# Mean of the SoLU output taken out in place on ScalarE, lower fp16 half made on GpSimd, and a new order of a round

## The chip, the cores and the metric

One core of one Trainium2 chip runs the whole program. The time is device microseconds of one execution. The engines are TensorE (PE in the rows), VectorE (DVE), ScalarE (ACT), GpSimd (POOL) and the DMA queues, the one of SyncE above all (SP).

## What is computed

Three stages in a row on 4608 tokens: chunked attention (chunks of 64, 8 heads of 64), a SoLU layer with layer norm (512 to 1024 to 512), and a mixture of 8 experts with one expert for each token (512 to 1024 to 512). The change is in the middle stage:

```python
h = x @ w_in
e = np.exp(h - h.max(-1))
solu = h * (e / (e.sum(-1) + 1e-9))
mu = solu.mean(-1); var = ((solu - mu) ** 2).mean(-1)
y = ((solu - mu) / np.sqrt(var + 1e-6) * g_ln) @ w_out
```

## The kernel before

Matmuls run in fp16 with every fp32 operand split in two halves: an upper half (the value rounded to fp16) and a lower half (the rest). A product takes three passes: upper by upper, upper by lower, lower by upper.

The first two reference stages are one loop over 36 tiles of 128 tokens, in software pipeline. Every engine works its instructions off in the order in which the program issues them. That order is written out by hand. `START` is a list of single steps for the first tiles (the weights are prepared in it too), with four tiles, 0 to 3, taken through SoLU. `BODY` is the list of one round. In round `i` the entry `um+0` calls step `um` for tile `i`, `mb-2` calls `mb` for tile `i-2`, and so on. The steps that matter here, with the engine that does each:

- `ld` SyncE loads raw q, k, v of a tile (L301, three buffers); `sc` GpSimd scales it (L311); `hq`, `hk` ScalarE and `lq`, `lk` GpSimd split it (L316, L320, L325, L332).
- `qk` TensorE scores; `mx` VectorE row max (L359); `su` VectorE subtracts it (L365); `ex` ScalarE exponential (L372); `sm` VectorE row sum and reciprocal (L377 to L379); `no` GpSimd normalizes (L384); `ph` ScalarE upper half (L406); `pl` VectorE lower half (L411, both inputs in SBUF); `pr` TensorE transpose; `pe` ScalarE eviction (L426); `pv` TensorE; `xh` ScalarE (L450) and `xl` VectorE (L457) split the attention output.
- `ma` TensorE `h` (L471); `hm` VectorE max of `h` (L477), which I call the max; `eh` ScalarE exponential with its sum (L484); `um` VectorE `u = h * e` with its sum, then two small multiplies for the mean, L493 and L494 (L491); `uh` ScalarE upper half of `u` minus mean, the mean as a bias (L513); `sq` ScalarE sum of squares of `u` minus mean (L499); `ul` VectorE lower half (L519); `ud` SyncE transposing DMA of both halves (L524, in `START` part of `ul`); `ss` GpSimd four tiny ops for the inverse deviation; `mb` TensorE second matmul (L537), which waits for the two eviction steps of the tile before since its PSUM tile has one buffer; `ev` ScalarE evictions (L551, L553) and `el` VectorE lower half of them (L559).
- `ro`, `rk`, `pa` rank the tokens by expert once in four tiles; `sA`, `sB` GpSimd scatter two tiles' rows to memory, in two rounds out of four.
- `ya`, `ys`, `yl` (and `yb`, `yt`, `ym`) split one piece of the experts' weights: ScalarE upper half (L274), VectorE lower half (L275, both inputs in SBUF), SyncE store and next load. From round 8 on every round has one piece; a round with `t % 9 < 5` has a second one, up to 40 pieces in all.

`u` and `e` have one buffer, `us` (the two halves of `u`) two, the transposed `uT` three; `h` and the scores have one PSUM tile each. In the last rounds GpSimd also issues three gathers (L183) that wait for scatters of the tiles before.

The third stage, the experts' matmuls (L93), follows; the change touches nothing in it.

Of the kernel before, what the change touches and what calls it, by code (L numbers as in the profile page):

```python
# [12 lines left out]
AF = mybir.ActivationFunctionType  # L13
ALU = mybir.AluOpType
# [5 lines left out]
NTOK, DM, DFF, NE, H, D = 4608, 512, 1024, 8, 8, 64  # L20
# [28 lines left out]

BODY = """  # L50
ev-3 el-3 pe+1 ph+2 pl+2 ya+0 ys+0 yl+0 ma+0 yb+0 yt+0 ym+0 pv+1 qk+3 hq+4 hk+4 xh+1 lq+4 sA+0 lk+4 sB+0 hm+0
eh+0 xl+1 sc+5 mx+3 um+0 uh+0 su+3 ex+3 sq+0 ul+0 mb-2 sm+3 ud+0 pr+2 rk-4 pa-4 ld+6 no+3 ss+0 ro-3
"""


# [6 lines left out]
S_E = 64.0  # L62
# [4 lines left out]
def tile_attention_solu_moe(  # L67
# [12 lines left out]
    V, A, G, T, SP = nc.vector, nc.scalar, nc.gpsimd, nc.tensor, nc.sync  # L80
# [155 lines left out]
    st = {}  # L236
# [51 lines left out]
    with ExitStack() as ab:  # L288
# [199 lines left out]
        def umul(t):  # L488
            (h, _), (e, se) = st.pop(("h", t)), st.pop(("e", t))
            u = u_p.tile([P, 1024], F32, tag="u", name="u", bufs=1)  # L490
            V.scalar_tensor_tensor(out=u, in0=h.rearrange("p a b -> p (a b)"), scalar=S_U / (S_X * S_WI), in1=e,  # L491
                                   op0=ALU.mult, op1=ALU.mult, accum_out=se[:, 1:2])
            V.tensor_scalar(se[:, 2:3], se[:, 1:2], -1.0 / DFF, None, op0=ALU.mult)  # L493
            V.tensor_scalar(se[:, 4:5], se[:, 1:2], -1.0 / (DFF * S_E), None, op0=ALU.mult)  # L494
            st["u", t] = (u, se, e)

        def stats(t):
            u, se, e = st["u", t]
            A.activation(e, u, AF.Square, bias=se[:, 4:5], scale=1.0 / S_E, accum_out=se[:, 3:4])  # L499
            st["se", t] = se  # L500

        def stats2(t):
# [4 lines left out]
            G.tensor_tensor(out=se[:, 7:8], in0=se[:, 6:7], in1=mhalf, op=ALU.pow)  # L507
            st["rr", t] = se

        def uhi(t):  # L510
            u, se, _ = st["u", t]
            us = u_p.tile([P, 2, 1024], F16, tag="us", name="us")
            A.activation(us[:, 0], u, AF.Identity, bias=se[:, 2:3])  # L513
            st["us", t] = us

        def ulo(t):
            u, se, _ = st["u", t]
            us = st["us", t]
            V.scalar_tensor_tensor(out=us[:, 1], in0=u, scalar=se[:, 2:3], in1=us[:, 0], op0=ALU.add, op1=ALU.subtract)  # L519

        def u_tr(t):
            us = st.pop(("us", t))
            uT = u_p.tile([P, 2, FC, P], F16, tag="uT", name="uT", bufs=3)
            SP.dma_start_transpose(out=uT.rearrange("p s f t -> p (s f) t"), in_=us.rearrange("p s f -> p (s f)"))  # L524
            st["uT", t] = uT
# [135 lines left out]
        def fetch(src, j):  # L661
            if wide:
                SP.dma_start(out=words[j].bitcast(src.dtype), in_=src)
            else:
                SP.dma_start(out=words[j][:, 0:1024].bitcast(F32), in_=src)
# [80 lines left out]
        def gate_split(_):  # L746
# [4 lines left out]

        steps = dict(
            ld=load, sc=scale_qv, hi=split_hi, lo=split_lo, qk=qk, mx=smax, su=ssub, ex=sexp, sm=ssum, no=snorm,
            pt=pt_pe, ph=pt_hi, pl=pt_lo, pv=pv, xh=xt_hi, xl=xt_lo, ma=m1, hm=hmax, eh=exph, um=umul, uh=uhi,
            sq=stats, ul=lambda t: (ulo(t), u_tr(t)), ss=stats2, mb=m2, ev=x2_ev, el=x2_lo,
            fi=lambda k: fetch(w_in[:, k], k), wa=win_f32, ws=win_scale, wh=win_hi, wl=win_lo,
            fo=lambda z: fetch(w_out[:, z], 2 + (z + 2) % 4), fg=consts, oa=wout_f32, os=wout_scale, oh=wout_hi, ol=wout_lo, wt=gate_tr, gs=gate_split, gm=gate_mm,
            gE=gate_end, wp=wpiece_load)
# [11 lines left out]
        def send():  # L770
            nonlocal sent
            if sent < routed:
                scatter(sent)
                sent += 1
# [39 lines left out]
        def early_pieces(t, n, f):  # L814
            if FIRST + 4 <= t < NT - 2 and done[0] < AHEAD and (n == 0 or t % 9 < 5):
                f()

        steps.update(
            ph=p_hi, pl=p_lo, pr=p_tr, pe=pt_ev, ul=ulo, ud=u_tr, hq=qv_hi, hk=k_hi,
            lq=qv_lo, lk=k_lo, mb=m2_tile, rk=rank, pa=place_rows,  # L820
            ro=route_rows, sA=lambda t: ok(t + 4) and send(), sB=lambda t: ok(t + 4) and send(),
            ya=lambda t: early_pieces(t, 0, piece_split), ys=lambda t: early_pieces(t, 0, piece_store),
# [2 lines left out]
        for i in range(FIRST, NT + 3):  # L825
            if i - FIRST < NX:
                G.memset(xs[i - FIRST], 0.0)
            for name in BODY.split():
                t = i + int(name[2:])
# [244 lines left out]
```

## Time and profile before

| what | us |
|---|---|
| median of 3 runs | 984.29 (980.61 to 989.86) |
| profiled execution | 983.6 |
| its span | 981.9 |
| TensorE busy | 887.6 (90%) |
| VectorE busy | 530.7 (54%) |
| ScalarE busy | 445.4 (45%) |
| GpSimd busy | 393.6 (40%) |

The rows below give a start in us from the span's start, a duration in us, the engine, the line of the kernel, the operation, output and inputs, and, where the engine had waited, how long and what ended the wait. An instruction can start on an engine a little before the one ahead of it has ended; so costs on a path are read from start to start.

### The profile page before, as it was taken

Reading aid. Unit: us, or ns where it says so; the run is one execution under the profiler, and the core shown is the slowest. Engines: PE = TensorE matmul, PEld = TensorE weight load, DVE = VectorE, ACT = ScalarE, POOL = GpSimd, SP = SyncE. Lnnn points to the kernel's source line nnn. Section 1 sums busy time; section 2 is a strip of 40 time slices with the busy share of each in tenths; the row PEclk is TensorE's granted clock in tenths of the full one; section 3 lists DMA queues with packets and bytes.
Section 4 is the critical chain, followed back from the end, with each engine's and each line's share of the span. In section 5 each row is a group of like instructions: output and inputs, shape, how many; then the busy total and the mean of one; then the engine's idle time right before and its main releaser. Section 6 shows DMA issues by size and latency. Waiting matters only on the chain.

```text
span 981.9 us, 26885 instructions
## 1 busy us (share of the span) xinstructions
PE 887.6 (90%) x11230; PEld 621.1 (63%) x11230; DVE 530.7 (54%) x966; ACT 445.4 (45%) x687; POOL 393.6 (40%) x503
## 2 busy tenths in 40 slices
PE   0476999989998999998998999998999999999997
PEld 0233666656666666665667776676767676777674
DVE  7996468898888888888963522222222221111111
ACT  3663367776777777777652122232222221112121
POOL 2765256656666666665443311112111211221120
PEclk9976999999999999999999999999999999999999
DMA  9377145898779987799679467979799853963234
GB/s 379 126 211 152 37 109 162 241 262 284 199 225 277 266 267 214 211 257 288 190 191 176 156 218 243 230 189 345 228 278 330 207 170 87 342 130 77 67 100 164
DMA packets 170145, 203.27 MB, mean 207 GB/s; under 512 B 131868, under 2 KB 131868, under 8 KB 164896
## 3 DMA queue, kind: packets, MB, share of 16 engines
q1 hardware_dynamic: 157280, 160.49, 57.6%
q0 software_dynamic: 9280, 28.40, 9.3%
q10 hardware_dynamic: 3456, 12.58, 3.7%
q8 instruction: 90, 1.47, 0.7%
q14 instruction: 39, 0.32, 0.1%
HBM read 244.40 MB, written 53.51 MB: 303 GB/s over the span
## 4 chain that ended last, share of the span: by engine, by line
PE 48%; DVE 24%; DMA 12%; issue 7%; ACT 5%; POOL 2%; SPq 1%; POOLq 0%; ACTq 0%; DVEq 0%
PE hc L93 17%; PE y L93 15%; PE h L471 9%; PE x L537 6%; DMA xT<-xs 4%; DVE us L519 4%; DVE ws L275 4%; DVE u L491 3%; DMA xs<-rows,c 3%; DVE mm L477 3%; ACT us L513 2%; DMA wsp<-ws 2%; ACT ws L274 1%; POOL p L384 1%; DVE ssum L377 1%
## 5 line engine op out<-in xcount | busy, mean ns | idle before, releaser
L93 PEld LDWEIGHTS <-w 128*128 128x128 f16 x3936 | 222.6, 98 | 29.1 <-DMA w<-wo 9.9
L207 DVE SCALAR_TENSOR_TENSOR hT<-hc,hT 128x512 f16<-128x512 f32 x78 | 53.7, 691 | 298.3 <-ACT hT L206 293.8
L93 PE MATMUL hc<-xT,w 128*128 128x128 f16 x3552 | 206.8, 220 | 6.6 <-DMA xT<-xs 5.5
L471 PE MATMUL h<-wi,xT 128*128 128x512 f16 x864 | 201.9, 392 | 10.7 <-DVE u L491 10.0
L93 PE MATMUL y<-w,hT 128*128 128x512 f16 x936 | 208.8, 379 | 2.5 <-ACT hT L206 2.1
L537 PE MATMUL x<-wo,uT 128*128 128x272 f16 x1728 | 204.1, 279 | 7.4 <-DVE row L559 7.4
L537 PEld LDWEIGHTS <-uT 128*128 128x128 f16 x1728 | 168.5, 99 | 35.2 <-issue 7.5
L227 POOL DMA_INDIRECT out_dram<-o,ix x40 | 40.7, 1018 | 328.8 <-ACT o L226 317.1
L471 PEld LDWEIGHTS <-xT 128*128 128x128 f16 x864 | 85.5, 101 | 112.9 <-issue 22.7
L93 PEld LDWEIGHTS <-hT 128*128 128x128 f16 x936 | 89.7, 98 | 104.6 <-ACT hT L206 2.6
L206 ACT ACTIVATE hT<-hc 128x512 f16<-128x512 f32 x78 | 46.4, 597 | 158.4 <-PE hc L93 153.5
L226 ACT ACTIVATE o<-y,xs 128x512 f32<-128x512 f32 x40 | 27.5, 687 | 151.8 <-PE y L93 141.2
L275 DVE SCALAR_TENSOR_TENSOR ws<-wf,ws 128x1024 f16<-128x1024 f32 x64 | 77.0, 1222 | 29.9 <-ACT ws L274 29.5
L325 POOL TENSOR_TENSOR qv<-raw,qv 128x1024 f16<-128x1024 f32 x33 | 76.9, 2332 | 26.8 <-ACT qv L316 26.8
L384 POOL TENSOR_TENSOR p<-p,ssum 128x512 f32<-128x512 f32 x36 | 37.9, 1054 | 106.0 <-DVE ssum L379 33.3
L274 ACT ACTIVATE ws<-wf 128x1024 f16<-128x1024 f32 x64 | 65.4, 1044 | 21.5 <-DMA wf<-in_w_dram 19.7
L519 DVE SCALAR_TENSOR_TENSOR us<-u,se,us 128x1024 f16<-128x1024 f32 x36 | 60.8, 1688 | 20.0 <-ACT us L513 19.5
L513 ACT ACTIVATE us<-u,se 128x1024 f16<-128x1024 f32 x36 | 41.3, 1148 | 48.0 <-DVE se L493 48.0
L484 ACT ACTIVATE e<-h,mm 128x1024 f32<-128x1024 f32 x36 | 40.1, 1114 | 45.2 <-DVE mm L478 44.9
L477 DVE TENSOR_REDUCE mm<-h 128x1 f32<-128x1024 f32 x36 | 43.8, 1218 | 15.3 <-PE h L471 15.3
L491 DVE SCALAR_TENSOR_TENSOR u<-h,e 128x1024 f32<-128x1024 f32 x36 | 44.1, 1225 | 7.4 <-ACT e L484 3.4
L332 POOL TENSOR_TENSOR k<-raw,k 128x512 f16<-128x512 f32 x34 | 41.4, 1218 | 13.0 <-ACT k L320 12.6
(177 smaller groups left out, 912.2 us busy)
## 6 DMA issues: line engine op xcount, KB each, us to landing
w<-wsp SPq DMA_DIRECT2D x152, 1024.0 KB
wf<-in_w_dram SPq DMA_DIRECT2D x64, 512.0 KB
raw<-in_qvk_dram SPq DMA_DIRECT2D x36, 768.0 KB
wsp<-ws SPq DMA_DIRECT2D x40, 512.0 KB
wsp<-ws ACTq DMA_DIRECT2D x24, 512.0 KB
w<-in_w_in_dram SPq DMA_DIRECT2D x4, 1024.0 KB
w<-wsp SPq DMA_DIRECT2D x8, 512.0 KB
wo<-in_w_out_dram SPq DMA_DIRECT2D x2, 1024.0 KB
```

Source lines behind the costliest of these rows:

```text
L93: T.matmul(ps, lhsT=l, rhs=r, start=(i == 0), stop=(i == n - 1))
L207: V.scalar_tensor_tensor(out=t[:, 1], in0=h, scalar=0.0, in1=t[:, 0], op0=ALU.max, op1=ALU.subtract)
L274: A.activation(s16[:, 0], f, AF.Copy, scale=S_E)
L275: V.scalar_tensor_tensor(out=s16[:, 1], in0=f, scalar=S_E, in1=s16[:, 0], op0=ALU.mult, op1=ALU.subtract)
L325: E.tensor_tensor(out=qv[:, 1], in0=raw, in1=qv[:, 0], op=ALU.subtract)
L384: (E or G).tensor_tensor(out=p, in0=p, in1=sm.unsqueeze(2).to_broadcast([P, H, D]), op=ALU.mult)
L471: T.matmul(h[:, j], lhsT=xT[:, a, kc], rhs=wi[b][:, n, f], start=(n + i == 0), stop=(n == KC - 1 and i == 2))
L477: V.tensor_reduce(mm[:, 0:1], h.rearrange("p a b -> p (a b)"), axis=AX.X, op=ALU.max)
L491: V.scalar_tensor_tensor(out=u, in0=h.rearrange("p a b -> p (a b)"), scalar=S_U / (S_X * S_WI), in1=e, op0=ALU.mult, op1=ALU.mult, accum_o ...
L513: A.activation(us[:, 0], u, AF.Identity, bias=se[:, 2:3])
L519: V.scalar_tensor_tensor(out=us[:, 1], in0=u, scalar=se[:, 2:3], in1=us[:, 0], op0=ALU.add, op1=ALU.subtract)
L537: T.matmul(x2[:, z, 0:n], lhsT=uT[:, a, f], rhs=wo[b][:, f, HD * (1 - z):HD * (1 - z) + n], start=(f + a + b == 0), stop=(last and a + b = ...
```

## The change

A new step `uc` on ScalarE takes the mean out of `u` in place. `uh` is then a plain copy to fp16. `sq` squares the centred `u` without a bias, so VectorE's second small multiply (L494) goes. (In `START`, `sq0` stands ahead of `uh0`, so that for tile 0 the sum of squares is of `u` with its mean still in it.) The lower half becomes a subtraction of two tensors; in `BODY` GpSimd does it, in `START` VectorE. In the round, `su` and `ex` come ahead of `um`, `sm` and `no` behind `um`, and then `uc uh sq ul`.

```diff
--- before.py
+++ after.py
@@ -49,7 +49,7 @@
 
 BODY = """
 ev-3 el-3 pe+1 ph+2 pl+2 ya+0 ys+0 yl+0 ma+0 yb+0 yt+0 ym+0 pv+1 qk+3 hq+4 hk+4 xh+1 lq+4 sA+0 lk+4 sB+0 hm+0
-eh+0 xl+1 sc+5 mx+3 um+0 uh+0 su+3 ex+3 sq+0 ul+0 mb-2 sm+3 ud+0 pr+2 rk-4 pa-4 ld+6 no+3 ss+0 ro-3
+eh+0 xl+1 sc+5 mx+3 su+3 ex+3 um+0 sm+3 no+3 uc+0 uh+0 sq+0 ul+0 mb-2 ud+0 pr+2 rk-4 pa-4 ld+6 ss+0 ro-3
 """
 
 
@@ -491,12 +491,11 @@
             V.scalar_tensor_tensor(out=u, in0=h.rearrange("p a b -> p (a b)"), scalar=S_U / (S_X * S_WI), in1=e,
                                    op0=ALU.mult, op1=ALU.mult, accum_out=se[:, 1:2])
             V.tensor_scalar(se[:, 2:3], se[:, 1:2], -1.0 / DFF, None, op0=ALU.mult)
-            V.tensor_scalar(se[:, 4:5], se[:, 1:2], -1.0 / (DFF * S_E), None, op0=ALU.mult)
             st["u", t] = (u, se, e)
 
         def stats(t):
             u, se, e = st["u", t]
-            A.activation(e, u, AF.Square, bias=se[:, 4:5], scale=1.0 / S_E, accum_out=se[:, 3:4])
+            A.activation(e, u, AF.Square, scale=1.0 / S_E, accum_out=se[:, 3:4])
             st["se", t] = se
 
         def stats2(t):
@@ -507,16 +506,19 @@
             G.tensor_tensor(out=se[:, 7:8], in0=se[:, 6:7], in1=mhalf, op=ALU.pow)
             st["rr", t] = se
 
+        def center(t):
+
+            u, se, _ = st["u", t]
+            A.activation(u, u, AF.Identity, bias=se[:, 2:3])
+
         def uhi(t):
-            u, se, _ = st["u", t]
             us = u_p.tile([P, 2, 1024], F16, tag="us", name="us")
-            A.activation(us[:, 0], u, AF.Identity, bias=se[:, 2:3])
+            A.activation(us[:, 0], st["u", t][0], AF.Copy)
             st["us", t] = us
 
-        def ulo(t):
-            u, se, _ = st["u", t]
+        def ulo(t, E=G):
             us = st["us", t]
-            V.scalar_tensor_tensor(out=us[:, 1], in0=u, scalar=se[:, 2:3], in1=us[:, 0], op0=ALU.add, op1=ALU.subtract)
+            E.tensor_tensor(out=us[:, 1], in0=st["u", t][0], in1=us[:, 0], op=ALU.subtract)
 
         def u_tr(t):
             us = st.pop(("us", t))
@@ -751,8 +753,8 @@
 
         steps = dict(
             ld=load, sc=scale_qv, hi=split_hi, lo=split_lo, qk=qk, mx=smax, su=ssub, ex=sexp, sm=ssum, no=snorm,
-            pt=pt_pe, ph=pt_hi, pl=pt_lo, pv=pv, xh=xt_hi, xl=xt_lo, ma=m1, hm=hmax, eh=exph, um=umul, uh=uhi,
-            sq=stats, ul=lambda t: (ulo(t), u_tr(t)), ss=stats2, mb=m2, ev=x2_ev, el=x2_lo,
+            pt=pt_pe, ph=pt_hi, pl=pt_lo, pv=pv, xh=xt_hi, xl=xt_lo, ma=m1, hm=hmax, eh=exph, um=umul,
+            uh=lambda t: (center(t), uhi(t)), sq=stats, ul=lambda t: (ulo(t, V), u_tr(t)), ss=stats2, mb=m2, ev=x2_ev, el=x2_lo,
             fi=lambda k: fetch(w_in[:, k], k), wa=win_f32, ws=win_scale, wh=win_hi, wl=win_lo,
             fo=lambda z: fetch(w_out[:, z], 2 + (z + 2) % 4), fg=consts, oa=wout_f32, os=wout_scale, oh=wout_hi, ol=wout_lo, wt=gate_tr, gs=gate_split, gm=gate_mm,
             gE=gate_end, wp=wpiece_load)
@@ -816,7 +818,7 @@
                 f()
 
         steps.update(
-            ph=p_hi, pl=p_lo, pr=p_tr, pe=pt_ev, ul=ulo, ud=u_tr, hq=qv_hi, hk=k_hi,
+            ph=p_hi, pl=p_lo, pr=p_tr, pe=pt_ev, uc=center, uh=uhi, ul=ulo, ud=u_tr, hq=qv_hi, hk=k_hi,
             lq=qv_lo, lk=k_lo, mb=m2_tile, rk=rank, pa=place_rows,
             ro=route_rows, sA=lambda t: ok(t + 4) and send(), sB=lambda t: ok(t + 4) and send(),
             ya=lambda t: early_pieces(t, 0, piece_split), ys=lambda t: early_pieces(t, 0, piece_store),
```

## Rows read from the trace of the kernel before

**Rows 1.** Windows: length, busy us of each engine (instructions), TensorE clock, DMA share, GB/s
```profile
118.42:154.62 36.20, 36.20 (x540) 24.90 (x541) 26.70 (x53) 25.02 (x39) 18.45 (x30) 1.00 0.41 100
166.73:471.50 304.77, 285.05 (x4179) 195.29 (x4178) 264.88 (x466) 226.86 (x348) 199.23 (x243) 1.00 0.84 248
```

**Rows 2.** Waits of TensorE, 110 to 480 us: total, times, longest
```profile
PE h L471 <- DVE u L491: 10.0, 9, 1.4
```

**Rows 3.** Timeline of VectorE, one round (tile 17 to tile 18)
```profile
285.02 1.22 DVE L477 TENSOR_REDUCE mm<-h 128x1 f32<-128x1024 f32 x1
...
286.34 0.68 DVE L457 SCALAR_TENSOR_TENSOR xT<-xps,xT 128x512 f16<-128x512 f32 x1
286.94 0.68 DVE L359 TENSOR_REDUCE sm<-s_ps 128x8 f32<-128x512 f32 x1
287.75 1.23 DVE L491 SCALAR_TENSOR_TENSOR u<-h,e 128x1024 f32<-128x1024 f32 x1
...
290.39 2.50 DVE L519 SCALAR_TENSOR_TENSOR us<-u,se,us 128x1024 f16<-128x1024 f32 x1 [0.56 <-ACT us L513]
...
295.82 0.69 DVE L411 SCALAR_TENSOR_TENSOR p<-p,p 128x512 f16<-128x512 f32 x1 [1.25 <-ACT p L406]
296.76 2.36 DVE L275 SCALAR_TENSOR_TENSOR ws<-wf,ws 128x1024 f16<-128x1024 f32 x2 [0.25 <-ACT ws L274]
299.04 1.22 DVE L477 TENSOR_REDUCE mm<-h 128x1 f32<-128x1024 f32 x1
```

**Rows 4.** Timeline of ScalarE, the same round
```profile
289.21 1.15 ACT L513 ACTIVATE us<-u,se 128x1024 f16<-128x1024 f32 x1 [1.49 <-DVE se L493]
...
290.79 1.13 ACT L499 ACTIVATE e<-u,se 128x1024 f32<-128x1024 f32 x1
...
291.92 0.25 ACT L551 ACTIVATE lgs<-x,se 128x16 f32<-128x16 f32 x1
...
292.64 1.01 ACT L426 ACTIVATE pt<-p16T 128x1024 f16<-128x1024 f16 x1
295.16 0.63 ACT L406 ACTIVATE p<-p 128x512 f16<-128x512 f32 x1 [1.50 <-POOL p L384]
295.69 1.99 ACT L274 ACTIVATE ws<-wf 128x1024 f16<-128x1024 f32 x2
297.59 1.04 ACT L316 ACTIVATE qv<-raw 128x1024 f16<-128x1024 f32 x1
```

**Rows 5.** Timeline of GpSimd, the same round
```profile
284.87 2.23 POOL L325 TENSOR_TENSOR qv<-raw,qv 128x1024 f16<-128x1024 f32 x1 [0.81 <-ACT qv L316]
...
294.08 1.04 POOL L384 TENSOR_TENSOR p<-p,ssum 128x512 f32<-128x512 f32 x1 [2.27 <-DVE ssum L379]
```

**Rows 6.** Timeline of VectorE in the start: `mx`, then `su` directly
```profile
80.80 0.64 DVE L359 TENSOR_REDUCE sm<-s_ps 128x8 f32<-128x512 f32 x1
81.55 0.69 DVE L365 TENSOR_TENSOR p<-s_ps,sm 128x512 f32<-128x512 f32 x1
```

**Rows 7.** Timeline of VectorE and of GpSimd at 20 us
```profile
20.48 2.15 DVE L748 SCALAR_TENSOR_TENSOR wg<-wgt,wg 128x64 f16<-128x64 f32 x1
...
20.00 2.55 POOL L693 TENSOR_TENSOR wi<-wf,wi 128x1024 f16<-128x1024 f32 x1
```

**Rows 8.** Timeline of VectorE in the start, 49 to 60 us
```profile
49.87 1.31 DVE L519 SCALAR_TENSOR_TENSOR us<-u,se,us 128x1024 f16<-128x1024 f32 x1 [0.34 <-ACT us L513]
...
58.16 0.69 DVE L401 SCALAR_TENSOR_TENSOR pt<-att,pt 128x512 f16<-128x512 f32 x1 [0.60 <-ACT pt L396]
```

**Rows 9.** Timeline of SyncE's queue, the round of rows 3
```profile
292.96 1.87 SPq L524 DMA_TRANSPOSE uT<-us  x1
294.92 1.02 SPq L301 DMA_DIRECT2D raw<-in_qvk_dram  x1
```

**Rows 10.** Timeline of TensorE and of GpSimd at the stage's end
```profile
525.81 7.16 PE L537 MATMUL x<-wo,uT 128*128 128x272 f16 x48 [3.30 <-DVE row L559]
...
511.35 1.08 POOL L183 DMA_INDIRECT xs<-rows,egx  x1 [6.45 <-DMA rows<-row,ix]
```

## The prediction

> **What bounds the kernel now.** I read first the windows by stretch. From tile 4 to tile 7 three rounds of the loop take 36.20 us, 12.07 each, and TensorE is busy in all of it [rows 1]: that is the pace of its matmuls. From the max of tile 8 to that of tile 31 the same loop takes 304.77 us for 23 rounds, 13.25 each, with TensorE busy in 285.05 [rows 1]. At the pace of 12.07 it would be 277.6, so 27.2 us are lost there. That is the most that any edit to this stage can give back. No engine is full (VectorE 264.88, ScalarE 226.86, GpSimd 199.23 of 304.77), so the limit is a ring of waits. The waits of TensorE name its way in: `h` stands behind VectorE's `u` [rows 2].
>
> The ring is read from the timeline of one round, tile 17 to 18, which is 14.02 us long [rows 3]. I count from the start of its max, H = 285.02. VectorE runs max, `xl`, `mx` and reaches `um` at 2.73. ScalarE starts `uh` 1.46 later [rows 4], VectorE starts `ul` 1.18 after that (290.39), and its row says that it waited for ScalarE. Then come `ul` and the sum of `sm`; GpSimd's `no` starts 3.69 after `ul` did [rows 5]. ScalarE's `ph` waited 1.50 for it and starts 1.08 after it, at 295.16. From there 0.53 to the weight piece `ya`, 1.07 until VectorE has it, 2.28 for two pieces, and the next max: 2.73 + 1.46 + 1.18 + 3.69 + 1.08 + 0.53 + 1.07 + 2.28 = 14.02. The sum closes, so this is the whole ring. By the code, 15 of the 23 rounds carry two weight pieces and 8 carry one; one piece less is 1.14.
>
> **The change part by part.**
>
> *The new ring.* With `ul` on GpSimd and `su`, `sm`, `no` ahead of the centring, `no` of a tile is done a round before its `ph`, so that wait of ScalarE goes. What is late next is ScalarE's own queue, which is in order: `uc`, `uh`, `sq`, the two evictions of `ev`, `pe`, `ph`, `ya`. I add it up from the same rows.
> - To `um`: max to `xl` 1.32, `xl` to `mx` 0.60 [rows 3]. `su` now follows `mx` directly and reads its result; such a pair stood 0.75 apart [rows 6]. `su` to `um` as `xl` to `mx`, 0.60. So `um` is at 3.27 instead of 2.73; `eh` has ended by then.
> - `um` to `uc` 1.46, as to `uh` now: 4.73.
> - `uc` is the old `uh` in another output type, with the same bias: 1.15 [rows 4]. `uh` reads what `uc` wrote, so I add 0.03 and take no overlap: 5.91. Bounds: 1.06 if they overlap, 1.25 if the wait between them is as long as in the pair of rows 6.
> - `uh` is now a copy without a bias. The same shape stands 0.95 apart (two in 1.90) [rows 4]: 6.86.
> - `sq` to `ev` is 1.13 with a bias from memory. Without it I take 1.03, since the biased 1024-element op took 1.15 and the unbiased one 1.04 [rows 4]; the upper bound is 1.13. 7.89.
> - `ev` to `pe` 0.72, `pe` 1.01, to `ph` at 9.62; 0.53 to `ya`, 1.07 to VectorE's half: 11.22. Two pieces 2.28: 13.50. One piece: 12.36.
>
> Both are above 12.07, so TensorE still waits. 15 x 13.50 + 8 x 12.36 = 301.4 against 304.77: **a gain of 3.4 us**. With the bounds on `uc` and `sq` a round moves by -0.12 to +0.17, and the gain is 6 to -0.5. The step saved two handovers to other engines and put one more pass of 1024 on ScalarE; the two almost cancel.
>
> *What leaves VectorE* (`ul`, 2.50 in this round and 1.31 where nothing disturbs it [rows 3, 8], and the small multiply) is worth nothing beyond that: VectorE waits for ScalarE at `pl` and `ws` already (1.25 and 0.25) and will wait longer.
>
> *`ul` on GpSimd.* A subtract of this shape took 2.23 there [rows 5]. 23 of them make 199.23 + 51 = 250 of 301 us, so GpSimd has the room. Its queue in this round, which has two scatters: free at 291.81 (`no` starts at 294.08 after 2.27 idle), H + 6.79. Then `no` to 7.87 and `ul`, whose input is there at 6.9, to 10.14. Behind it stand `ss` (needed three rounds on), the small sums of `ro`, and the next `lq` (not before 12.2): hidden. VectorE's `pl`, the next op with two inputs in SBUF, starts when `ph` ends, at 10.27. That margin of 0.13 matters. A VectorE op of 64 elements with both inputs in SBUF took 2.15 and ended with the GpSimd subtract that ran beside it [rows 7], so what overlaps is lost in full. VectorE's `ws` behind `pl` has two such inputs as well. The Trainium skill (SBUF — State Buffer, § Who interferes with whom) says the same and more: a VectorE instruction with two SBUF inputs and a GpSimd one that reads SBUF exclude each other, and the one that starts first keeps the port. By that rule `ul`, which starts first, would hold `pl` back, as by the row. I charge 0 to 0.2 a round, together 0 to 4.6, and take **1 us**.
>
> *Queues moved past.* SP's transposing load of `us` waits for `ul`: 292.96, H + 7.94 now, H + 10.2 then [rows 9]. The load of the next `raw` stands behind it and goes from H + 9.90 to 12.2. Its reader on GpSimd ends at 6.79 of the next round, so load and reader have 8.1 us instead of 10.9. No row shows that it needs more, so I take nothing. The transposed tile is read two rounds on.
>
> *Start* (tiles 0 to 3, where the lower half stays on VectorE). VectorE waited 0.34 for ScalarE at the first `ul`, so 1.18 of `uc` comes on top; the next wait for ScalarE, 0.60, takes up part of it [rows 8]. Between 0 and 1.2: **0.6 us**.
>
> *End of the stage.* The last-but-one `mb` waits 3.30 for VectorE's `el` [rows 10], which needs `ev`, behind `uc` on ScalarE: 0 to 1.18, I take **0.5**. Also, GpSimd stands still until 511.35 for its first gather, 6.45 of it for scatters [rows 10], and two more gathers follow; `ul` of tile 34 is queued behind them, some 5 to 7 us later than on VectorE. Its transpose is wanted by that same `mb` at 525.81. I take nothing; the upper bound is about 6.
>
> The second stage (experts) has none of the changed lines.
>
> **Sum:** -3.4 + 1.0 + 0.6 + 0.5 = -1.3 us. The profiled execution took 983.6 (span 981.9), so 982.3; the median of the three runs is 0.7 higher, 983.0. I say 982.5.
>
> **The rivals.**
> - *TensorE's own pace is reached* (faster). If the ring through ScalarE were shorter than 12.07, all 27.2 us would return: 983.6 - 27.2 + 1.1 = 957.5; half of it, 971. For it: both handovers named as waits go. Against it: the new queue sums to 12.36 and 13.50, and to get under 12.07 with two pieces 1.4 us must be wrong. Chance 0.17.
> - *The shared port* (slower). If GpSimd's `ul` ends later than 10.5 of its round, VectorE's `pl`, then `ws`, then the max stand behind it, and each us of lateness is one on the ring (after 0.2 of slack ahead of `ws`). At 11.5 in every round: 23 x 1.0 = 23, 1005; at 11.0, 994. What would make it late is the `raw` load behind the transpose, or subtracts slower than 2.23. For it: the margin of 0.13 and the port rule. Against it: by the code half of the rounds have no scatters and leave GpSimd more room. Chance 0.22.
> - *The end of the stage pays* for the gathers: +6, 988. It is inside 1%; 0.08 of the chance of no change.
>
> **How the numbers follow.** My forecast with its near neighbours, 0.61; faster 0.17; slower 0.22. About 1% (974 to 994) is what a measurement of this kernel can tell from no change. Likeliest alone: 977 to 990 (bounds of `uc`, `sq`, port, start and end). Since cases of both signs hold 0.39, the range for 8 in 10 reaches half-way into each: 970 to 1000. Part of the slower case (up to 0.5 us of lateness) stays inside 1%, part of my own range's upper end leaves it, so I keep 0.17, 0.60 and 0.23.
>
> **What would show it.** Right: rounds of about 13.5 and 12.4 between maxes; no wait of ScalarE for GpSimd at `ph`, but VectorE waiting over 2 us for ScalarE's `ev` and again at `pl`; TensorE's waits for `u` still there with two pieces. Wrong: rounds of 12.07 (the ring was shorter); `pl` or `ws` much longer than 0.69 and 1.2 (port); `sc` on GpSimd waiting for a load; `mb` of tile 34 waiting for its transpose.

## The result, and the profile after

| | before | after |
|---|---|---|
| median of 7 runs each, us | 984.29 (980.61 to 989.86) | 992.87 (990.11 to 999.19) |
| ratio, 95% interval | | 1.0098 [1.0071, 1.0124] |
| span of the profiled execution, us | 981.9 | 990.1 |
| start of the max (L477): tile 4 / 8 / 31 | 118.42 / 166.73 / 471.50 | 117.73 / 167.04 / 476.93 |
| first expert matmul on TensorE (`hc`), us | 532.80 | 541.22 |

The change made the kernel 1% slower; the forecast was 982.5, no change that can be measured. The starts of the max say where the time went. Up to tile 8 the changed kernel is 0.31 later. From tile 8 to tile 31 it loses 5.12 more (309.89 against 304.77), and between tile 31 and the first expert matmul another 2.99 (64.29 against 61.30). That is 8.42 us, and the second stage keeps it: the spans differ by 8.2.

Windows of the changed kernel, to set against [rows 1] (length, busy us of each engine with instructions, TensorE clock, DMA share, GB/s):

```profile
117.73:153.92 36.19, 36.19 (x540) 24.90 (x540) 23.50 (x46) 27.92 (x42) 23.45 (x27) 1.00 0.31 77
167.04:476.93 309.89, 285.68 (x4083) 195.51 (x4084) 244.66 (x421) 249.06 (x371) 263.04 (x264) 1.00 0.90 246
```

As intended, work left VectorE (264.88 to 244.66 us) and went to GpSimd (199.23 to 263.04); ScalarE has 22 us more. Still none of the three is full.

**The ring that was forecast is there.** This is one round with two weight pieces that nothing disturbs, tile 20 to 21, as [rows 3, 4] show one of before; first VectorE, then ScalarE:

```profile
328.64 1.22 DVE L477 TENSOR_REDUCE mm<-h 128x1 f32<-128x1024 f32 x1
...
331.89 1.22 DVE L491 SCALAR_TENSOR_TENSOR u<-h,e 128x1024 f32<-128x1024 f32 x1
...
338.87 0.69 DVE L411 SCALAR_TENSOR_TENSOR p<-p,p 128x512 f16<-128x512 f32 x1 [0.68 <-ACT p L406]
339.82 2.36 DVE L275 SCALAR_TENSOR_TENSOR ws<-wf,ws 128x1024 f16<-128x1024 f32 x2 [0.25 <-ACT ws L274]
```

```profile
333.39 1.15 ACT L512 ACTIVATE u<-u,se 128x1024 f32<-128x1024 f32 x1 [0.76 <-DVE se L493]
334.57 1.06 ACT L516 ACTIVATE us<-u 128x1024 f16<-128x1024 f32 x1
335.53 1.04 ACT L498 ACTIVATE e<-u 128x1024 f32<-128x1024 f32 x1
...
338.20 0.64 ACT L406 ACTIVATE p<-p 128x512 f16<-128x512 f32 x1
338.72 2.01 ACT L274 ACTIVATE ws<-wf 128x1024 f16<-128x1024 f32 x2
```

Counted from 328.64: `um` 3.25 (forecast 3.27), `uc` 4.75 (4.73), `uh` 5.93 (5.91), `sq` 6.89 (6.86), `ph` 9.56 (9.62), the weight pieces on VectorE 11.18 (11.22). The next max is at 342.09, a round of 13.45 (13.50). Rounds with one piece that nothing disturbs take 12.31 to 12.35 (12.36). With 13.45 and 12.33 the stretch would be 15 x 13.45 + 8 x 12.33 = 300.4, a gain of 4.4 us over before. It took 309.89, so **9.5 us sit in disturbed rounds**.

**What a disturbed round looks like.** The round from tile 14 to 15 has one piece and took 13.66. SyncE's queue, GpSimd, VectorE:

```profile
245.74 3.56 SPq L526 DMA_TRANSPOSE uT<-us  x1
249.35 0.57 SPq L301 DMA_DIRECT2D raw<-in_qvk_dram  x1
```

```profile
255.51 1.04 POOL L311 TENSOR_SCALAR raw<-raw 128x1024 f32<-128x1024 f32 x1 [3.91 <-DMA raw<-in_qvk_dram]
256.52 1.04 POOL L384 TENSOR_TENSOR p<-p,ssum 128x512 f32<-128x512 f32 x1
257.52 2.13 POOL L521 TENSOR_TENSOR us<-u,us 128x1024 f16<-128x1024 f32 x1
...
269.87 2.13 POOL L521 TENSOR_TENSOR us<-u,us 128x1024 f16<-128x1024 f32 x1
```

```profile
258.25 1.94 DVE L411 SCALAR_TENSOR_TENSOR p<-p,p 128x512 f16<-128x512 f32 x1 [1.11 <-ACT p L406]
...
269.98 2.05 DVE L624 SCALAR_TENSOR_TENSOR rs<-rs 128x4 f32<-128x4 f32 x1
```

Read them in this order. The transposing transfer (L526) starts when GpSimd's subtract of that tile ends (243.57 for 2.14), and its issue took 3.56. The input load of a later tile (L301) stands behind it on SyncE's queue. The load could be read 6.16 us after its own issue began, and GpSimd's scale (L311) waited 3.91 for it. `no` (L384) and the new subtract `ul` (L521) came behind the scale, so `ul` ran from 257.52 to 259.65, and VectorE's `pl` (L411) beside it took 1.94, not 0.69. A round later an operation of four columns (L624) took 2.05 and ended with the subtract. From 167 to 470 us, the groups by line of the changed kernel (count, busy us, mean ns, idle before):

```profile
L411 DVE SCALAR_TENSOR_TENSOR p<-p,p 128x512 f16<-128x512 f32 x22 | 20.5, 931 | 11.5 <-ACT p L406 11.5
L624 DVE SCALAR_TENSOR_TENSOR rs<-rs 128x4 f32<-128x4 f32 x5 | 4.6, 916 | 0.2
L582 DVE TENSOR_TENSOR oh<-rw,rs 128x32 f16<-128x32 f32 x5 | 3.1, 620 | 0.2
L311 POOL TENSOR_SCALAR raw<-raw 128x1024 f32<-128x1024 f32 x23 | 24.2, 1050 | 23.6 <-DMA raw<-in_qvk_dram 17.4 <-DVE rs L581 2.7 <-DVE rw L579 2.3
```

Of the 17.4 us that L311 waits for loads, 13.7 lie in the 11 rounds without scatters. Not all of the surplus goes through VectorE's held operations: in the longest round (tile 29 to 30, 14.75) ScalarE's second weight piece waits 1.38 for a weight store, which is issued behind that transfer and load (four such waits from 110 to 480 us, 2.8 in all; none with the input load first, below).

**The end of the stage**, to set against [rows 10] (GpSimd, VectorE, TensorE):

```profile
521.32 1.08 POOL L183 DMA_INDIRECT xs<-rows,egx  x1 [7.40 <-DMA rows<-row,ix]
...
525.06 2.13 POOL L521 TENSOR_TENSOR us<-u,us 128x1024 f16<-128x1024 f32 x1
```

```profile
527.23 1.23 DVE L491 SCALAR_TENSOR_TENSOR u<-h,e 128x1024 f32<-128x1024 f32 x1 [2.61 <-POOL us L521]
```

```profile
534.31 7.07 PE L539 MATMUL x<-wo,uT 128*128 128x272 f16 x48 [4.41 <-DVE row L561]
```

`ul` of tile 34 stands behind three gathers on GpSimd. `u` has one buffer, so VectorE's product of tile 35 waits 2.61 for that subtract. The last-but-one `mb` then waits 4.41 for `el`, where it waited 3.30.

### The profile page after: what moved, and what is told of

Its sections match the earlier page's. It is cut to its first block, busy times and chain, and to the rows that moved or that the text cites. A ratio compares the mean times of both kernels' runs of the same rounds, so it can differ in the third digit from the quotient of the medians.

```text
span 990.1 us, 26912 instructions
## 1 busy us (share of the span) xinstructions
PE 886.2 (90%) x11230; PEld 620.3 (63%) x11230; DVE 502.5 (51%) x898; ACT 480.7 (49%) x723; POOL 475.4 (48%) x535
## 4 chain that ended last, share of the span: by engine, by line
PE 38%; DVE 20%; DMA 16%; ACT 11%; issue 7%; POOL 6%; SPq 1%; POOLq 0%; ACTq 0%; DVEq 0%
PE hc L93 17%; PE y L93 15%; DMA wsp<-ws 7%; DVE ws L275 3%; DMA xT<-xs 3%; DVE mm L477 3%; PE h L471 3%; PE x L539 3%; DVE u L491 2%; DMA wf<-in_w_dram 2%; ACT u L512 2%; ACT us L516 2%; ACT ws L274 2%; ACT e L498 2%; POOL us L521 1%
## 5 line engine op out<-in xcount | busy, mean ns | idle before, releaser
L521 POOL TENSOR_TENSOR us<-u,us 128x1024 f16<-128x1024 f32 x32 | 68.2, 2130 | 5.7 <-ACT us L516 5.5
L561 DVE SCALAR_TENSOR_TENSOR row<-x,se,row 128x512 f16<-128x512 f32 x36 | 26.8, 745 | 72.6 <-ACT row L555 72.4
L512 ACT ACTIVATE u<-u,se 128x1024 f32<-128x1024 f32 x36 | 41.3, 1147 | 28.2 <-DVE se L493 25.9
L311 POOL TENSOR_SCALAR raw<-raw 128x1024 f32<-128x1024 f32 x32 | 35.3, 1103 | 37.4 <-DMA raw<-in_qvk_dram 31.2
L384 POOL TENSOR_TENSOR p<-p,ssum 128x512 f32<-128x512 f32 x36 | 37.9, 1053 | 23.8 <-DVE ssum L379 15.7
L477 DVE TENSOR_REDUCE mm<-h 128x1 f32<-128x1024 f32 x36 | 43.8, 1217 | 10.7 <-PE h L471 10.7
```

The costliest lines, as they stand in the source:

```text
L477: V.tensor_reduce(mm[:, 0:1], h.rearrange("p a b -> p (a b)"), axis=AX.X, op=ALU.max)
L512: A.activation(u, u, AF.Identity, bias=se[:, 2:3])
L521: E.tensor_tensor(out=us[:, 1], in0=st["u", t][0], in1=us[:, 0], op=ALU.subtract)
```

## The experiments

Ratios are to the kernel before, run on the same chip beside each.

| run | median, us | ratio [95% interval] | tile 8 to 31, us |
|---|---|---|---|
| before | 984.29 | | 304.77 |
| after | 992.87 | 1.0098 [1.0071, 1.0124] | 309.89 |
| order alone | 969.29 | 0.9857 [0.9809, 0.9906] | 290.66 |
| after, subtract on VectorE | 983.46 | 0.9996 [0.9971, 1.0021] | 300.37 |
| after, subtract on VectorE for the last tiles | 991.35 | 1.0092 [1.0060, 1.0124] | |
| after, ranking step earlier | 1011.12 | 1.0312 [1.0263, 1.0362] | |
| after, input load first on its queue | 982.69 | 1.0009 [0.9976, 1.0042] | 301.52 |
| order alone, scale behind the multiply | 969.76 | 0.9852 [0.9807, 0.9898] | 291.49 |
| before, with the centring | 997.74 | 1.0132 [1.0095, 1.0169] | 316.53 |
| order alone, load first | 970.07 | 0.9854 [0.9815, 0.9893] | 290.05 |
| the same, scale between the input subtracts | 960.08 | 0.9783 [0.9736, 0.9830] | 282.14 |
| the same, second scatter later | 963.14 | 0.9794 [0.9749, 0.9840] | 282.69 |

**The order alone.** The kernel before with the new order of the round; no centring, `ul` on VectorE.

```diff
-eh+0 xl+1 sc+5 mx+3 um+0 uh+0 su+3 ex+3 sq+0 ul+0 mb-2 sm+3 ud+0 pr+2 rk-4 pa-4 ld+6 no+3 ss+0 ro-3
+eh+0 xl+1 sc+5 mx+3 su+3 ex+3 um+0 sm+3 no+3 uh+0 sq+0 ul+0 mb-2 ud+0 pr+2 rk-4 pa-4 ld+6 ss+0 ro-3
```

> The kernel before with the new order of a round alone (su, ex ahead of um; sm, no ahead of uh); no centring in place, the lower half as before on VectorE. Theory (the ring through ScalarE's in-order queue sets the round): um 3.24 after the max, uh 1.46 on, sq 1.06, ev 1.13, pe 0.72, ph 1.01, ya 0.53, VectorE's half 1.07, so 10.2, with two pieces 12.5 and with one 11.4, which is under TensorE's 12.07. From tile 8 to tile 31 about 15 x 12.5 + 8 x 12.07 = 284 instead of 304.8, the whole kernel 963 to 968. Rival (the order itself brings nothing or is what harms; the time lies in GpSimd's or in the DMAs' part): 980 to 990, rounds of 13 and more.

969.29: the new order by itself is worth 1.4%, and the change gives all of it back. The theory had asked for more (about 284 us for the stretch, and it took 290.66); "A faster order" below shows what held it up.

**The subtract back on VectorE.** The changed kernel, with `ul` of the round on VectorE again.

```diff
-            ph=p_hi, pl=p_lo, pr=p_tr, pe=pt_ev, uc=center, uh=uhi, ul=ulo, ud=u_tr, hq=qv_hi, hk=k_hi,
+            ph=p_hi, pl=p_lo, pr=p_tr, pe=pt_ev, uc=center, uh=uhi, ul=lambda t: ulo(t, V), ud=u_tr, hq=qv_hi, hk=k_hi,
```

> The changed kernel with the lower half of u back on VectorE in the loop; centring and new order stay. Theory (two separate costs: the centring pass keeps the ring at 13.45 and 12.33; GpSimd's subtract adds port, SyncE-queue and end-of-stage costs on top): rounds of 13.45 and 12.33 without the longer ones, tile 8 to 31 about 303 to 304 instead of 309.9, end of the stage 3 shorter, 982 to 985. Rival (the centring pass or the order makes all of the loss, GpSimd none): 990 to 993. Rival (GpSimd's subtract is all that keeps the gain away): 965 to 972.

983.46, and the stretch takes 300.37, what the undisturbed ring makes (300.4); that it fits to 0.1 is chance, since the quiet rounds here are 13.39 and 12.25 and the placings add 0.2 in five of them. So the whole surplus of 9.5 us comes with GpSimd's subtract. The order alone and this run differ in the centring only (with the plain copy and the unbiased square, in `START` too): it costs 14.2 us, 9.7 of them between tiles 8 and 31. The sum of the parts, in ratios: order -1.4%, centring +1.4%, subtract on GpSimd +1.0%.

**The subtract on VectorE at the end only** (tiles 33 to 35).

```diff
-            ph=p_hi, pl=p_lo, pr=p_tr, pe=pt_ev, uc=center, uh=uhi, ul=ulo, ud=u_tr, hq=qv_hi, hk=k_hi,
+            ph=p_hi, pl=p_lo, pr=p_tr, pe=pt_ev, uc=center, uh=uhi, ul=lambda t: ulo(t, V if t >= 33 else G), ud=u_tr, hq=qv_hi, hk=k_hi,
```

> The changed kernel with the lower half on VectorE for tiles 33 to 35 alone, so that no subtract stands behind the three gathers of GpSimd. Theory: um of tile 35 no longer waits 2.6 for the subtract of tile 34 (u has one buffer); the last-but-one mb starts 2.5 to 3.5 sooner against the max of tile 31, the kernel 989 to 990.5. Rival (the second stage waits for its loads anyway and takes the gain back): 992 to 994.

991.35, an interval that covers the changed kernel's ratio. VectorE's product of tile 35 no longer waits for GpSimd, and the first expert matmul is 1.7 us earlier (539.56), but the span is no shorter (990.9). The median lies between the two ranges that were expected and decides for neither. What the end loses to the gathers is real on TensorE, but getting part of it back doesn't show in the time.

**The ranking step earlier.** In five rounds VectorE's placing (`pa`) waits for ScalarE's exponentials of `rk`, which stand behind the centring. Here `rk` is put ahead of `uc`.

```diff
-... sm+3 no+3 uc+0 uh+0 sq+0 ul+0 mb-2 ud+0 pr+2 rk-4 pa-4 ...
+... sm+3 no+3 rk-4 uc+0 uh+0 sq+0 ul+0 mb-2 ud+0 pr+2 pa-4 ...
```

> The changed kernel with the ranking step (its matmuls and the two small exponentials on ScalarE) ahead of uc, so that VectorE's place step does not wait behind uc, uh and sq. Theory: the five rounds behind a place step (before the max of tiles 8, 12, 16, 20, 24 and 28) lose their surplus of 0.2 to 1.3, together about 4; 988 to 990. Rival (VectorE has room there, the surplus is the ring's own): 992 to 994.

1011.12, far from every expectation. `rk` also holds two matmuls. Moved ahead of `mb`, they wait in TensorE's order for a PSUM tile that VectorE frees late (waits of TensorE, 110 to 480 us: total, times, longest):

```profile
PE rt L599 <- DVE p L365: 27.8, 6, 6.0
```

The edit tested something else than meant. That the placing's wait is cheap is shown by two other runs. With the input load first the wait is there (1.27 us in the round from 206.38); with the subtract on VectorE it isn't, as that subtract stands ahead of the placing. In both, the rounds with a placing that nothing else disturbs are 0.2 us longer than the others.

**The input load first.** The changed kernel; the load of tile i+6 stands ahead of the transposing transfer of tile i on SyncE's queue. Nothing that an engine computes is moved.

```diff
-... ul+0 mb-2 ud+0 pr+2 rk-4 pa-4 ld+6 ss+0 ro-3
+... ul+0 mb-2 ld+6 ud+0 pr+2 rk-4 pa-4 ss+0 ro-3
```

> The changed kernel with one step moved: the load of tile i+6's input (L301) is issued on SyncE's queue ahead of the transposing transfer of tile i (L526), not behind it. No operation of an engine changes. Theory 1, the queue: in the changed kernel SyncE stands at L526 until GpSimd's subtract is done, so the next input load leaves late, GpSimd's scale L311 waits for it (17.4 us in 15 waits between 167 and 470), its multiply L384 and the next subtract L521 are late, and they then meet VectorE's L411 and L624. With the load first L311's wait goes to under 2 us, L411 goes back from 0.93 to about 0.70 us, and tile 8 to tile 31 takes 301 to 304 us (the ring alone is 300.4; 309.9 in the changed kernel); the time is 984 to 987 us. Theory 2, the shared port alone: GpSimd is busy 263 of the 310 us of that stretch whatever the load does, its subtract meets VectorE's operations as before, L411 stays at 0.9 us, the stretch takes 307 us or more and the time stays within 3 us of 992.9.

982.69: the whole loss is gone. Windows, then the same groups by line:

```profile
165.99:467.51 301.52, 285.21 (x4137) 195.20 (x4124) 247.49 (x421) 248.81 (x372) 263.05 (x264) 1.00 0.88 250
```

```profile
L411 DVE SCALAR_TENSOR_TENSOR p<-p,p 128x512 f16<-128x512 f32 x23 | 17.4, 756 | 9.0 <-ACT p L406 9.0
L624 DVE SCALAR_TENSOR_TENSOR rs<-rs 128x4 f32<-128x4 f32 x5 | 0.8, 164 | 0.2
L582 DVE TENSOR_TENSOR oh<-rw,rs 128x32 f16<-128x32 f32 x6 | 12.3, 2052 | 0.2
L311 POOL TENSOR_SCALAR raw<-raw 128x1024 f32<-128x1024 f32 x23 | 24.2, 1052 | 0.4
```

GpSimd is busy for the same 263 us, so it was not too full: it was late. With the input there in time, L311 waits for no load, L624 is back at 0.16 us and L411 nearly at 0.69. L411 and L624 together are 7.6 us shorter over the stretch, and the stretch is 8.4 shorter.

That doesn't mean that VectorE is held less. It is busy for 247.49 us here and for 244.66 in the changed kernel, and L582 takes 12.3 for six in place of 3.1 for five. What changed is which operations are held. The round from tile 14 to 15 again, now 12.31 and not 13.66; the subtract runs from 252.88 to 255.01:

```profile
253.00 2.06 DVE L582 TENSOR_TENSOR oh<-rw,rs 128x32 f16<-128x32 f32 x1
...
255.61 0.75 DVE L561 SCALAR_TENSOR_TENSOR row<-x,se,row 128x512 f16<-128x512 f32 x1
256.27 0.68 DVE L411 SCALAR_TENSOR_TENSOR p<-p,p 128x512 f16<-128x512 f32 x1
```

In the changed kernel VectorE waited for ScalarE here, 1.71 at L561 and 1.11 at L411, and was then held in L411. Now it is held earlier, and the hold fills those waits. The queue is shown as the trigger. That most of the time goes at the shared port, in operations with no such wait behind them, is read from these rows; no run takes the port away and leaves the lateness.

**Centring in the old order.** The kernel before with the centring, the plain copy and the unbiased square; `ul` on VectorE.

```diff
-eh+0 xl+1 sc+5 mx+3 um+0 uh+0 su+3 ...
+eh+0 xl+1 sc+5 mx+3 um+0 uc+0 uh+0 su+3 ...
```

> The kernel before in its old order, with ScalarE's in-place centring and the plain copy for the upper half; the subtract of the lower half stays on VectorE. In the new order this same step (the run with the subtract on VectorE against the order alone) costs 14.2 us. Theory 1, the ring: the added operation of 1.15 us stands between the product u and the upper half, and in the old order the upper half stands on the chain from h to the next product in every round, so each of the 23 rounds between tile 8 and tile 31 is 1.0 to 1.2 us longer: that stretch goes from 304.8 to about 329 us, and the time to 1007 to 1012 us. Theory 2: the old order has slack there (VectorE waits 12.3 us for the upper half in that stretch but GpSimd and TensorE are not full), so that only some 0.4 us of a round is paid, as in the new order: 995 to 1000 us.

997.74, 1.3% above before, nearly what centring costs in the new order (1.4 points). The stretch takes 316.53, 11.8 more or 0.51 a round on the mean. But no round pays the mean. The 11 rounds without scatters are each 1.02 to 1.04 longer, nearly all of the 1.15 that `uc` lasts; of the 12 with scatters 11 are unchanged to 0.02, and the first is 0.35 longer. VectorE's lower half tells why. First a round without scatters (tile 19 to 20), before and in this run; then, in this run, a round with two (tile 17 to 18):

```profile
317.93 1.28 DVE L519 SCALAR_TENSOR_TENSOR us<-u,se,us 128x1024 f16<-128x1024 f32 x1 [0.56 <-ACT us L513]
```

```profile
324.77 1.22 DVE L521 TENSOR_TENSOR us<-u,us 128x1024 f16<-128x1024 f32 x1 [1.71 <-ACT us L516]
```

```profile
296.19 1.42 DVE L521 TENSOR_TENSOR us<-u,us 128x1024 f16<-128x1024 f32 x1 [1.70 <-ACT us L516]
```

The last one is to be set against the 2.50 of [rows 3], the same round of before. There the lower half was ready 5.38 after the max and was held beside GpSimd's scatter issue and scale; with the centring it is ready at 6.46. It ends 7.87 and 7.88 after the max. The delay went into a hold that was there already.

**A faster order.** VectorE's small L378 (0.17 us in before) took 0.88 on the mean in the order alone. There it runs beside GpSimd's scale in the rounds with scatters:

```profile
322.57 1.51 DVE L378 TENSOR_SCALAR ssum<-ssum 128x8 f32<-128x8 f32 x1
324.23 1.25 DVE L519 SCALAR_TENSOR_TENSOR us<-u,se,us 128x1024 f16<-128x1024 f32 x1
```

```profile
322.99 1.06 POOL L311 TENSOR_SCALAR raw<-raw 128x1024 f32<-128x1024 f32 x1
324.46 1.92 POOL L384 TENSOR_TENSOR p<-p,ssum 128x512 f32<-128x512 f32 x1 [0.42 <-DVE ssum L379]
```

First the scale was put behind the multiply:

```diff
-eh+0 xl+1 sc+5 mx+3 su+3 ex+3 um+0 sm+3 no+3 uh+0 ...
+eh+0 xl+1 mx+3 su+3 ex+3 um+0 sm+3 no+3 sc+5 uh+0 ...
```

> The new order alone, without the centring and with the subtract on VectorE (969.3 us), and in it GpSimd's scale of the next input (L311) put behind its multiply L384 in place of ahead of it. Theory 1, the port: in the new order VectorE's tiny L378 runs beside the scale and takes 0.88 us on the mean (0.17 in the kernel before), up to 1.5, and the multiply stands behind the scale as well; with the scale behind the multiply L378 goes back to 0.2 to 0.3 us, the multiply comes about 1 us earlier, and a round with two weight pieces falls from 13.07 us to between 12.1 and 12.5 (12.1 is TensorE's own work in such a round). 15 such rounds give 9 to 15 us: 955 to 961. Theory 2: the round with two pieces is held by VectorE's own work (11.7 us busy in a round) and TensorE's pace, both near it already, or the scale meets VectorE's next operation instead: 13.0 and 966 to 970 us.

969.76, no gain. L378 fell to 0.24 and five of the 15 rounds with two pieces to 12.39, as the first theory said; but in others the scale now met `ul`, and eight take 13.3 to 13.7:

```profile
309.75 2.15 DVE L519 SCALAR_TENSOR_TENSOR us<-u,se,us 128x1024 f16<-128x1024 f32 x1
```

```profile
309.78 1.04 POOL L384 TENSOR_TENSOR p<-p,ssum 128x512 f32<-128x512 f32 x1 [2.42 <-ACT us L513]
310.79 2.02 POOL L311 TENSOR_SCALAR raw<-raw 128x1024 f32<-128x1024 f32 x1
```

The collision had moved. The next three runs change the order alone step by step: the load first; then also the scale between GpSimd's two input subtracts; then also the second scatter behind the multiply.

```diff
-... ul+0 mb-2 ud+0 pr+2 rk-4 pa-4 ld+6 ss+0 ro-3
+... ul+0 mb-2 ld+6 ud+0 pr+2 rk-4 pa-4 ss+0 ro-3
```

> The new order alone (no centring, subtract on VectorE, 969.3 us), with the input load L301 ahead of the transposing transfer on SyncE's queue. Theory 1, the queue matters for the new order itself: L311 waits 13.8 us in 10 waits for its input between 110 and 480; without these the multiply L384 comes sooner and tile 8 to tile 31 falls from 290.7 to 285 to 288 us, the time to 964 to 967 us. Theory 2, the queue hurts only where GpSimd is nearly full: in the order alone GpSimd has room, the waits change places, and the time stays within 2 us of 969.3.

970.07: without GpSimd's subtract the queue costs nothing that can be seen. The second theory holds.

```diff
-... lq+4 sA+0 lk+4 sB+0 hm+0 eh+0 xl+1 sc+5 mx+3 ...
+... lq+4 sc+5 sA+0 lk+4 sB+0 hm+0 eh+0 xl+1 mx+3 ...
```

> As the run before it (new order alone, input load first), and GpSimd's scale L311 moved from behind its two input subtracts to between them, where VectorE reads its operands from PSUM. Theory 1, the port: VectorE's L378 goes from 0.88 to 0.2 us, and the scale meets no operation of VectorE with two operands in SBUF, so that neither the rounds with 13.07 us (order alone) nor those with 13.4 to 13.7 us (scale behind the multiply) are left: rounds of 12.1 to 12.4 us, tile 8 to tile 31 in 278 to 283 us, the time 957 to 962 us. Theory 2: what L378 loses is not on the chain that sets the round, or the second input subtract and the multiply are now late by the scale's 1.05 us: 966 to 972 us.

**960.08, 2.2% below before** and the lowest median of the study. L378 takes 0.22 on the mean, TensorE's waits for `u` fall from 7.7 to 1.0 us, and TensorE is busy nearly throughout:

```profile
165.52:447.66 282.14, 281.74 (x4176) 194.14 (x4172) 256.97 (x465) 227.53 (x348) 211.44 (x245) 1.00 0.92 267
```

```diff
-... lk+4 sB+0 hm+0 ... no+3 uh+0 ...
+... lk+4 hm+0 ... no+3 sB+0 uh+0 ...
```

> As the run before it, and GpSimd's second scatter issue (sB) moved behind the multiply L384, so that the multiply stands behind one operation of 0.98 us less. If the multiply's start is what TensorE's next transposes wait for, the rounds with two weight pieces are 0.3 to 0.9 us shorter than in the run before it (15 of them: 4 to 13 us less). If VectorE's own work sets those rounds by then, nothing changes (within 2 us of the run before it), or the scatter issue now delays the four small operations of L504 to L507 and nothing is seen of it.

963.14, the stretch as in the run before it (282.69): with TensorE at its pace, an earlier multiply buys nothing. The intervals of the two runs overlap, so the 3 us between their medians say nothing. Their profiled executions are 8.0 us apart, yet the first expert matmuls only 0.74 (509.73 and 510.47): that difference arose behind this stage, where neither run changes anything.

## Why the prediction was wrong

- *The ring* was right in mechanism and size: 13.45 and 12.33 against 13.50 and 12.36, and 300.4 against 301.4 for the stretch. That the saved handovers and the added pass of ScalarE "almost cancel" is shown too: the order is worth 1.4%, the centring costs as much.
- *SP's queue* is **the step that failed**. I saw the load move later with the transposing transfer ahead of it, counted 8.1 us where before had 10.9, and took nothing since "No row shows that it needs more". Three terms were mis-sized. I put the load at 12.2 of its round; in the round from 274.52 it was issued at 288.12, at 13.60, since the transfer ahead of it took 3.05 to issue and not 1.87 [rows 9]. Where GpSimd waited for it between tiles 8 and 31, the load took 5.8 to 6.8 us from its issue until GpSimd started on it. And I took the reader's time (6.79) from a round with two scatters; in a round without them GpSimd was ready at 251.60, 4.0 after that round's max. There the load comes too late by 3.91. The trace of before had rows for two of the three. A load that GpSimd waited for in the start was issued at 55.40 and had landed 5.43 later. And in the 11 rounds without scatters the scale starts 3.2 to 3.7 after the max, as here in the round from 312.56:

```profile
316.00 1.04 POOL L311 TENSOR_SCALAR raw<-raw 128x1024 f32<-128x1024 f32 x1
```

  In those rounds before had 6.2 to 8.2 us from the load's issue to its reader, not 10.9. A load that leaves 2.3 us later is, by my estimate from these numbers, late in most of them.
- *The shared port.* The rival named both the trigger (the load behind the transpose) and the place (`pl`, behind `ul`), and that is what happened, at 9.5 us at the most, under the 11 to 23 it was priced at, since only some rounds are hit. I gave it 0.22, because I had judged its trigger by the step above. My reason against it, that the rounds without scatters leave GpSimd more room, pointed the wrong way: there GpSimd is ready earliest and waits longest for the load. The term in my sum, 1 us with a bound of 4.6, was too low. Four-column operations such as L624 were missing from it: of the short operations I had only `pl` in mind, but a tiny one is blocked for as long (in two of the five rounds with a placing, 3.8 us together). The Trainium skill (SBUF — State Buffer, § Who interferes with whom) excludes a VectorE instruction with two SBUF inputs while GpSimd reads SBUF; the trace agrees, 2.05 us beside a subtract of 2.13.
- *The end* was taken as 0.5 with a bound of 6 and is 3.0 in the first expert matmul. The gathers did hold back `ul` of tile 34; the way it hurt (one buffer of `u`) was not seen. With the subtract on VectorE there, 1.8 of it came back (62.50 from tile 31 on), and the span stayed where it was. Where the other 1.2 come from is open.
- *Start*: +0.6 forecast; tile 4 is 0.69 earlier and tile 8 is 0.31 later. One profile can't decide this: over the six runs with the new start the max of tile 4 comes at 117.25 to 118.66 (mean 118.07), over the six with the old one at 116.52 to 118.42 (mean 117.39). The means fit the forecast; the spread is wider than the difference.
- *TensorE's pace*, the rival on the other side, needs less on the ring than the centring leaves. Without the centring, and with the scale out of VectorE's way, it came about: 282.14 us for 23 rounds, 12.27 each. The bound that I took for it (12.07, so 277.6) was close.
- The run with the load first is the kernel that I had predicted: 982.69 against 982.5. That is in part luck: its end is 4.0 us longer than before's, and its start is 0.74 and the stretch 3.25 shorter.

## What to carry to other kernels

A transfer queued behind one that waits for a slower engine is late by that engine's delay, and so is everything that its data feeds; work out the reader's time in the round where the reader is earliest, not in the one at hand, and put loads that wait for nothing ahead. GpSimd's work was free for VectorE where VectorE read PSUM, and beside a reduction with one SBUF input (L377: 0.68 at 182.55 in the fastest kernel, with a subtract of GpSimd running beside all of it); operations with two SBUF inputs were held, and so were the small L378 and L623 with one. Place it by the operands of the neighbours, not by who is idle, and where a hold can't be avoided, ahead of a wait that takes it up. A pass added on the engine that carries the ring cost nearly all of its duration in the rounds where nothing else held the chain and nothing in the others: a mean over rounds hides this.

## What the runs showed of the hardware

- A VectorE operation can be held by GpSimd's *issue* of an indirect transfer. In the run with the scale behind the multiply, L378 started at 322.61, took 0.36 instead of 0.17 and so ended at 322.97; GpSimd's scatter issue beside it ran from 322.00 for 0.99, until 322.99. In the order alone L378 started at 322.57, before the scale (322.99), and was held until the scale's end (324.05): a scatter issue ran ahead of that scale. In the changed kernel too L378 took 0.41 from 279.80, with an issue beside it until 280.24. The same pattern fits `ul` in [rows 3]: it took 2.50 from 290.39, with a scatter issue from 289.73 for 0.98 and the scale from 290.75 for 1.06 beside it. That the issue is what held it was not tried.
- Both sides are held. `ul` from 324.23 kept its 1.25 us, and GpSimd's multiply, from 324.46, took 1.92 instead of 1.04. At 309.75 and 309.78 it was VectorE that waited, although it started 0.03 earlier.
- In the run with the ranking step earlier TensorE stood for 6.04 us and then got a lower granted clock, so that the next `mb` took 8.21 us instead of 5.57 (window of that kernel, and TensorE):

```profile
213.20:220.00 6.80, 6.79 (x39) 4.91 (x40) 6.53 (x14) 4.07 (x7) 6.11 (x7) 0.59 0.87 352
```

```profile
213.28 8.21 PE L539 MATMUL x<-wo,uT 128*128 128x272 f16 x48
```

A granted clock of 0.59 is a mean over that window, most of it at the lower of the two levels (1.2 GHz of 2.4); the window after it has 1.00. A wait of TensorE there costs more than its length.
